# Which operand is held in the array: the product of w_out and phi in an attention, MoE and soft-MoE kernel

## The chip, the cores and the metric

The kernel runs on one core of a Trainium2 chip. The metric is the device time of one execution in microseconds (us); the time before is the median of 3 runs.

## The reference

Three blocks stand one behind the other. The first is causal attention over 4 batches, 12 heads, 448 tokens and a head size of 64. Its result, laid out as x with 1792 rows and 768 columns, goes through a feed-forward block without gates, and its output through a soft mixture of 8 experts with 4 slots each:

```python
h = x @ w_in                      # 768 -> 2048
x = np.maximum(0.01 * h, h) @ w_out   # 2048 -> 768
logits = x @ phi                  # 768 -> 32 slots
d = softmax(logits over tokens); c = softmax(logits over slots)
slot_input = d.T @ x
slot_out = per expert: relu(slot_input @ w1) @ w2
out = c @ slot_out
```

The weights w_in and w_out come in 64-bit floating point and are turned into 32-bit numbers on the chip; everything that the change touches is 32-bit.

## The kernel before, in words

The logits need only `g @ (w_out @ phi)`, so the kernel forms the product `wprime = w_out @ phi` once, 2048 rows by 32 columns, in 16 units f of 128 rows each. A unit is the work of the generator `prep_out`: it takes the raw rows of w_out, converts them on ScalarE, VectorE and GpSimd, stores the converted rows to HBM for a later stage (`wsc`), and turns them with six transposes on TensorE (`wt_ps`, copied by ScalarE to `wt`: six blocks `wt[:, c]` with the model dimension on the partitions). Then come the steps that the change is about. In the kernel before, `phi_sb[:, c]` (128 rows, 32 columns) is the weight and `wt[:, c]` (128 columns) passes through. The six products go to three groups of 32 output partitions, so that three of them can be in the array side by side, two behind each other in each group. That leaves three partial sums of the turned result in `wp_ps` (96 by 128). ScalarE copies them to `w4`. After a `yield AFTER` a further product with `w4` as the weight and a stack of identity blocks passing through adds the three parts and turns the result back (`wf_ps`, 128 by 32), and ScalarE copies it to `wprime[:, f]`.

The order of the work is written by hand on TensorE: every `mm` and `tr` is tied behind the one before, in the order of the program. ScalarE is tied in the same way from the second stage on. The orders of VectorE and GpSimd are left to a planner that works from estimated times. The program runs in stages of 18 slots (`stage`). In each slot one third of the attention of a head pair is issued, then one step of each running generator of the phase BEFORE, then one column block f of the up-projection `H` (18 products, `up`), then one step of each running generator of the phase AFTER, the oldest first. A `yield AFTER` in `prep_out` therefore puts what follows it into the next slot. Units 0 to 9 of w_out are prepared in the third stage (from about 227 to 321 us), units 10 to 15 in the fourth (343 to 432 us).

The tiles of `ps_tr` share one set of PSUM buffers (tag "tr"), two of them in these stages: `wt_ps` (two tiles for a unit), `wp_ps`, `wf_ps`, the turned maxima of the attention (`mps`), its denominators (`dn`), and the logits (`L`). A product into such a tile waits until the buffer's last reader is done. `logits` reads `wprime` as a weight, from about 368 us on. After the fourth stage come the rest of the up-projection with the combination of the logits, and then the expert block, which reads w1 and w2 from HBM.

Of the kernel before, what the change touches and what calls it, by code (L numbers as in the profile page):

```python
# [10 lines left out]
F32 = mybir.dt.float32  # L11
# [23 lines left out]
def tile_attn_moe_softmoe(ctx: ExitStack, tc: tile.TileContext, q, k, v, w_in, w_out, phi, w1, w2, out, dbg=None):  # L35
# [6 lines left out]
    NS = phi.shape[1]  # L42
# [4 lines left out]
    NP = H // 2  # L47
# [12 lines left out]
    istack = const.tile([128, 128], F32, name="istack")  # L60
# [6 lines left out]
    wprime = const.tile([128, NF, NS], F32, name="wprime")  # L67
    phi_sb = const.tile([128, NP, NS], F32, name="phi_sb")
# [19 lines left out]
    def ps_tr(name, shape=(128, 512)):  # L88
        return psum.tile(list(shape), F32, tag="tr", bufs=TR[0], name=name)
# [27 lines left out]
    scalar = Scalar()  # L117
# [13 lines left out]
    mm = partial(in_order, nc.tensor.matmul)  # L131
# [43 lines left out]
    for x, u in enumerate(units):  # L175
        stage = 0 if x < EARLY[0] else 1 if x < whole else 2
        order += [u + (h, stage) for h in ((0, 1) if stage == 2 else (None,))]
    waiting = list(order)
    pools = [None, None, None]
# [34 lines left out]
    def to_f32(u, absmax=None):  # L214

        raw = raws.pop(u)
        kind, f, h, stage = u
        nm = f"{kind}{f}_{h}"
        w = DM if h is None else DH
        hw, lw = raw[..., 1], raw[..., 0]  # L220
        _, nt, ns = BUFS[stage]
        t = pools[stage].tile([128, w], F32, tag="cv_t", bufs=nt, name="cv_" + nm)
        sg = pools[stage].tile([128, w], BF16, tag="cv_s", bufs=ns, name="cs_" + nm)
        ti = t.bitcast(I32)
        scalar.activation(t, hw.bitcast(F32), AF.Abs, scale=2.0**-112)
        scalar.activation(sg, hw.bitcast(F32), AF.Sign)
        if absmax is not None:
            nc.vector.tensor_reduce(absmax, t, AX.X, ALU.max)
        nc.vector.tensor_scalar(ti, ti, 3, None, ALU.logical_shift_left)
        nc.vector.scalar_tensor_tensor(ti, lw, 29, ti, ALU.logical_shift_right, ALU.bitwise_or)  # L230
        load_raw()
        return t, sg
# [28 lines left out]
    def prep_out(us):  # L261

        f, stage = us[0][1], us[0][3]
        wos = []
        for u in us:
            wo, sg = to_f32(u)
            nc.gpsimd.tensor_tensor(wo, wo, sg, ALU.mult)  # L267
            c0 = DH * (u[2] or 0)
            nc.sync.dma_start(
                wsc.rearrange("(k g a p) n -> k a g p n", k=4, g=4, a=4)[f // 4, f % 4][:, :, c0 : c0 + wo.shape[1]], wo  # L270
            )
            wos.append((wo, c0))
            if u is not us[-1]:
                yield BEFORE
        if len(us) == 1:
            yield AFTER
        yield AFTER
        wt = pools[stage].tile([128, NP, 128], F32, tag="wt", bufs=1, name=f"wt{f}")
        for h in (0, 1):
            wo, c0 = wos[h % len(wos)]  # L280
            ps = ps_tr(f"wt_ps{f}_{h}", (128, 3, 128))
            for j in range(3):
                c = 128 * (3 * h + j) - c0
                tr(ps[:, j], wo[:, c : c + 128], ident)
            scalar.copy(wt[:, 3 * h : 3 * h + 3], ps)
            if h == 0 and len(us) > 1:
                yield AFTER
        yield AFTER
        psw = ps_tr(f"wp_ps{f}", (96, 128))
        for c in range(NP):  # L290
            j = c % 3
            mm(
                psw[32 * j : 32 * j + 32], phi_sb[:, c], wt[:, c], start=c < 3, stop=c >= 3, skip_group_check=True
            )
        w4 = pools[stage].tile([96, 128], F32, tag="w4", bufs=1, name=f"w4_{f}")
        scalar.copy(w4, psw)
        yield AFTER
        psf = ps_tr(f"wf_ps{f}", (128, NS))
        mm(psf, w4, istack[:96, :NS], start=True, stop=True)
        scalar.copy(wprime[:, f], psf)  # L300
        ready.add(us[0][:2])

    ready = set()
    BEFORE, AFTER = "before", "after"
# [12 lines left out]
    def prep_start():  # L317
        u = units[started[0]]
        started[0] += 1
        us = [x for x in order if x[:2] == u]  # L320
        g = prep_in(us[0]) if u[0] == "i" else prep_out(us)
        running.append([g, next(g)])
# [557 lines left out]
    if True:  # L880
# [123 lines left out]
        for c in range(4):  # L1004
            wo = loaded.pop(("wo", c))
            for h in range(2):
                for t in range(4):
                    nc.tensor.matmul(
                        psi[h][32 * t : 32 * t + 32], gdt[:, c, t], wo[:, t, 384 * h : 384 * (h + 1)],
                        start=c == 0, stop=c == 3, skip_group_check=True,  # L1010
# [18 lines left out]
        for e in range(E):  # L1029
            ph = ps2(f"ph{e}", (128, 256), tag="h", bufs=4)  # L1030
            for hf in range(2):
                wt = loaded.pop(("w1", (e, hf)))
                for t in range(3):
                    rows = wt[:, t].rearrange("k (p t) -> k p t", t=8)
                    for g in range(4):
# [3 lines left out]
                            start=hf == 0 and t == 0, stop=hf == 1 and t == 2, skip_group_check=True,  # L1039
# [87 lines left out]
        for x, (t0, nt, c0, cols) in enumerate(pieces):  # L1127
            if x:
                load_next(1)
            wt = loaded.pop(("w2", x))  # L1130
# [8 lines left out]
            for h in heads:  # L1139
                for t in range(nt):  # L1140
# [3 lines left out]
                        start=t0 + t < 4, stop=t0 + t >= 8 * E - 4, skip_group_check=True,  # L1144
# [65 lines left out]
```

## Time and profile before

| | |
|---|---|
| median of 3 runs | 646.38 us (645.07 to 647.01) |
| the profiled execution | 642.54 us |
| its span, first to last instruction | 640.8 us |
| mean granted TensorE clock | 0.985 of full speed |
| TensorE products busy (PE) | 573.1 us, 89% |
| weight loads busy (PEld) | 326.0 us, 51% |
| VectorE (DVE) | 382.7 us, 60% |
| ScalarE (ACT) | 289.5 us, 45% |
| GpSimd (POOL) | 238.1 us, 37% |

The profile tells for one execution what each engine did and when. PE is a product's passage, PEld the load of its weight, which can lie beside the product before it. A product of 32-bit numbers appears as two loads and two passages. The duration of a passage contains the way through the array; how closely passages follow each other is read from their starts. A share of busy time is a mean over stages with different limits.

### The profile page before, as it was taken

Reading aid. Unit: us, or ns where it says so; the run is one execution under the profiler, and the core shown is the slowest. Engines: PE = TensorE matmul, PEld = TensorE weight load, DVE = VectorE, ACT = ScalarE, POOL = GpSimd, SP = SyncE. Lnnn points to the kernel's source line nnn. Section 1 sums busy time; section 2 is a strip of 40 time slices with the busy share of each in tenths; the row PEclk is TensorE's granted clock in tenths of the full one; section 3 lists DMA queues with packets and bytes.
Section 4 is the critical chain, followed back from the end, with each engine's and each line's share of the span. In section 5 each row is a group of like instructions: output and inputs, shape, how many; then the busy total and the mean of one; then the engine's idle time right before and its main releaser. Section 6 shows DMA issues by size and latency. Waiting matters only on the chain.

```text
span 640.8 us, 12316 instructions
## 1 busy us (share of the span) xinstructions
PE 573.1 (89%) x4810; PEld 326.0 (51%) x4810; DVE 382.7 (60%) x900; ACT 289.5 (45%) x570; POOL 238.1 (37%) x247
## 2 busy tenths in 40 slices
PE   3688888997899999999999989999999998998564
PEld 2455555654555566555555555554344445554233
DVE  5868757998984666787578778424657423001013
ACT  2566755678665566657445654432022112011012
POOL 5186883388586373444435434430000000000000
PEclk9989989999999999999999999999999998999998
DMA  9942227755662467764343322208969539999999
GB/s 180 288 121 59 60 65 199 216 154 124 163 183 73 86 199 201 202 174 108 98 118 97 111 68 72 61 13 278 358 230 420 202 132 418 410 419 425 408 325 326
DMA packets 123698, 125.68 MB, mean 196 GB/s; under 512 B 84216, under 2 KB 113912, under 8 KB 120056
## 3 DMA queue, kind: packets, MB, share of 16 engines
q1 hardware_dynamic: 123640, 124.90, 61.3%
q8 instruction: 38, 0.62, 0.4%
q14 instruction: 20, 0.16, 0.1%
HBM read 105.74 MB, written 19.14 MB: 195 GB/s over the span
## 4 chain that ended last, share of the span: by engine, by line
PE 61%; DMA 12%; DVE 9%; POOL 9%; ACT 4%; issue 3%; SPq 1%; POOLq 0%; ACTq 0%; DVEq 0%
PE H L102 29%; DMA w<-in_moe_w_dram 8%; PE O L102 5%; PE T L102 4%; PE g_acc L102 3%; PE L L102 2%; PE dn L102 2%; PE S L102 2%; DMA raw_i_None<-in_moe_w_in_dram 2%; DVE cv_i_None L230 2%; PE ph L1036 2%; PE wt_ps L102 2%; POOL tsum L484 2%; ACT P L113 2%; POOL w L258 2%
## 5 line engine op out<-in xcount | busy, mean ns | idle before, releaser
L102 PE MATMUL H<-x,w 128*128 128x448 f16 x1152 | 229.1, 353 | 0.7 <-ACT g L113 0.7
L102 PEld LDWEIGHTS <-w 128*128 128x128 f16 x1152 | 110.1, 99 | 111.7 <-issue 18.2
L435 DVE CUSTOM_DVE_ANT_0 junk<-S,mask 112x224 bf16<-112x224 f32 (+3 forms) x192 | 84.9, 442 | 53.7 <-PE S L102 50.7
L513 DVE RECIPROCAL rs<-rs 128x224 f32<-128x224 f32 x36 | 53.3, 1523 | 25.9 <-ACT rs L113 25.9
L475 POOL TENSOR_SCALAR_AFFINE_SELECT P<-P 112x448 f32<-112x448 f32 x48 | 34.7, 724 | 88.6 <-ACT P L113 52.9
L113 ACT ACTIVATE P<-T 112x672 f32<-112x672 f32 (+1 forms) x72 | 56.9, 792 | 21.2 <-PE T L102 20.2
L102 PE MATMUL T<-qkt 64*112 64x336 f32 (+3 forms) x576 | 59.4, 318 | 4.1 <-ACT P L113 3.3
L113 ACT ACTIVATE g<-H,iv 128x448 f32<-128x448 f32 x48 | 30.4, 634 | 64.2 <-PE H L102 45.8
L102 PE MATMUL O<-P,v 112*64 112x448 f32 (+3 forms) x384 | 54.4, 426 | 3.9 <-POOL P L475 3.9
L102 PEld LDWEIGHTS T<-qkt 64*112 64x112 f32 x576 | 42.2, 178 | 14.2 <-issue 5.7
L484 POOL TENSOR_TENSOR tsum<-tsum,P 112x448 f32<-112x448 f32 (+1 forms) x48 | 47.3, 986 | 1.8
L102 PEld LDWEIGHTS O<-P,v 112*64 112x64 f32 x384 | 26.2, 142 | 29.9 <-issue 13.0
L480 POOL TENSOR_TENSOR tsum<-P 112x672 f32<-112x672 f32 x24 | 39.1, 1630 | 1.8
L102 PE MATMUL S<-qkt 64*112 64x224 f32 (+3 forms) x192 | 31.3, 365 | 8.4 <-DVE mxe L435 3.7
L1028 POOL MEMSET hz<- 128x256 f32 x2 | 0.6, 311 | 97.7 <-PE g_acc L102 97.7
L113 ACT ACTIVATE g_spare<-H,iv 128x448 f32<-128x448 f32 x16 | 10.1, 634 | 56.8 <-PE H L102 56.8
L113 ACT ACTIVATE mr<-mps,own 128x112 fp32r<-128x112 f32 x96 | 26.2, 361 | 16.7 <-PE mps L102 16.7
L113 ACT COPY rs<-dn 128x448 f32<-128x448 f32 x18 | 9.6, 532 | 51.9 <-PE dn L102 51.9
L102 PE MATMUL T<-mr,onesr 64*112 64x448 f32 (+1 forms) x192 | 30.7, 316 | 2.5 <-ACT mr L113 2.5
L249 POOL TENSOR_TENSOR cv_i_None<-cv_i_None,cs_i_None 128x768 f32<-128x768 f32 x16 | 28.5, 1784 | 11.6 <-ACT cs_i_None L113 11.6
L267 POOL TENSOR_TENSOR cv_o_None<-cv_o_None,cs_o_None 128x768 f32<-128x768 f32 x10 | 16.5, 1646 | 40.7 <-DVE cv_o_None L230 21.5
L258 POOL TENSOR_TENSOR w<-cv_i_None,w 128x768 f16<-128x768 f32 x16 | 26.8, 1674 | 10.4 <-ACT w L113 10.4
(179 smaller groups left out, 907.6 us busy)
## 6 DMA issues: line engine op xcount, KB each, us to landing
w<-in_moe_w_dram SPq DMA_DIRECT2D x31, 1536.0 KB, 14.9
raw_i_None<-in_moe_w_in_dram SPq DMA_DIRECT2D x16, 768.0 KB, 4.8
raw_o_None<-in_moe_w_out_dram SPq DMA_DIRECT2D x10, 768.0 KB, 5.7
g_far<-g SPq DMA_DIRECT2D x32, 224.0 KB, 4.3
gb<-g_far SPq DMA_DIRECT2D x8, 896.0 KB, 6.9
wo<-wsc SPq DMA_DIRECT2D x4, 1536.0 KB, 7.7
v<-in_v_dram SPq DMA_DIRECT2D x24, 224.0 KB, 3.5
out_dram<-ob SPq DMA_DIRECT2D x14, 384.0 KB, 3.7
```

The source lines that it names most:

```text
L102: op(*args, **kwargs)
L113: op(*args, **kwargs)
L230: nc.vector.scalar_tensor_tensor(ti, lw, 29, ti, ALU.logical_shift_right, ALU.bitwise_or)
L249: nc.gpsimd.tensor_tensor(t, t, sg, ALU.mult)
L258: nc.gpsimd.tensor_tensor(lo, w, hi, ALU.subtract)
L267: nc.gpsimd.tensor_tensor(wo, wo, sg, ALU.mult)
L435: nc.vector.tensor_tensor_reduce(out=junk[:, :w], in0=ps[:, a, at : at + w], in1=mask[:, S - w :], scale=-1.0, scalar=3e38, op0=ALU.add, o ...
L475: nc.gpsimd.affine_select(out=d, in_=d, compare_op=ALU.is_ge, fill=0.0, base=0, pattern=[[0, 4], [1, CP]], channel_multiplier=-1,)
L480: nc.gpsimd.tensor_tensor(tsum[:CP], p[0][:CP, :, 0, CP:], p[0][:CP, :, 1, : S - CP], ALU.add)
L484: nc.gpsimd.tensor_tensor(y, y, p[1][:CP, :, j, : S - CP * (j + 2)], ALU.add)
L513: nc.vector.reciprocal(rs[:, c : c + S // 2], rs[:, c : c + S // 2])
L1036: nc.tensor.matmul(ph[32 * g : 32 * g + 32].rearrange("s (p u) -> s p u", u=2), sit[:, 3 * hf + t], rows[:, :, 2 * g : 2 * g + 2], start=h ...
```

## The change

The turned block of w_out becomes the weight (128 columns, 32-bit) and `phi_sb[:, c]` (32 columns) passes through. All six products add up in one PSUM tile of 128 by 32, which already has the orientation of `wprime[:, f]`; ScalarE copies it there. The tile `w4`, its copy, the product with the identity stack, the tile `wf_ps` and one `yield AFTER` go.

```diff
         yield AFTER
-        psw = ps_tr(f"wp_ps{f}", (96, 128))
+        psw = ps_tr(f"wp_ps{f}", (128, NS))
         for c in range(NP):
-            j = c % 3
-            mm(
-                psw[32 * j : 32 * j + 32], phi_sb[:, c], wt[:, c], start=c < 3, stop=c >= 3, skip_group_check=True
-            )
-        w4 = pools[stage].tile([96, 128], F32, tag="w4", bufs=1, name=f"w4_{f}")
-        scalar.copy(w4, psw)
-        yield AFTER
-        psf = ps_tr(f"wf_ps{f}", (128, NS))
-        mm(psf, w4, istack[:96, :NS], start=True, stop=True)
-        scalar.copy(wprime[:, f], psf)
+            mm(psw, wt[:, c], phi_sb[:, c], start=c == 0, stop=c == NP - 1)
+        scalar.copy(wprime[:, f], psw)
         ready.add(us[0][:2])
```

## Rows read from the trace of the kernel before

**Rows 1.** Windows: engines' busy us in a stretch (instructions), clock, DMA.

```profile
230.00:290.00 60.00, 57.99 (x463) 34.85 (x463) 42.60 (x82) 37.31 (x78) 28.90 (x24) 1.00 0.65 190
290.00:325.00 35.00, 34.14 (x273) 20.33 (x273) 25.00 (x50) 19.80 (x43) 15.82 (x14) 1.00 0.43 102
...
345.00:385.00 40.00, 38.18 (x305) 22.00 (x304) 30.48 (x69) 23.55 (x52) 18.92 (x19) 1.00 0.28 81
385.00:435.00 50.00, 48.01 (x362) 26.89 (x360) 26.77 (x47) 21.62 (x50) 20.35 (x22) 1.00 0.20 57
```

**Rows 2.** The chain that ended last, in order of time: start, us, what.

```profile
309.73 0.97 PE wt_ps L102 x6
...
565.20 49.82 DMA w<-in_moe_w_dram x2
```

**Rows 3.** Timeline of PE, 231 to 236 us: start, us, instructions merged.

```profile
231.30 3.57 PE L102 MATMUL H<-x,w 128*128 128x448 f16 x18
234.80 0.64 PE L102 MATMUL wp_ps<-wt,phi_sb 128*32 128x128 f32 x12
235.36 0.99 PE L102 MATMUL wt_ps<-ident,cv_o_None 128*128 128x128 f32 x6
236.28 0.36 PE L102 MATMUL S<-qkt 64*112 64x224 f32 x2
```

**Rows 4.** Timeline of PE, 239 to 244 us; in brackets a wait and its releaser.

```profile
239.52 3.57 PE L102 MATMUL H<-x,w 128*128 128x448 f16 x18
242.93 0.31 PE L102 MATMUL wf_ps<-istack,w 96*128 96x32 f32 x2
243.16 0.64 PE L102 MATMUL wp_ps<-wt,phi_sb 128*32 128x128 f32 x12
243.98 0.85 PE L102 MATMUL wt_ps<-ident,cv_o_None 128*128 128x128 f32 x6 [0.18 <-ACT wprime L113]
```

**Rows 5.** Timeline of PE: products of one weight form, two overlapping stretches near 537 us.

```profile
536.15 1.73 PE L102 MATMUL pgt<-istack,ge 128*128 128x32 f32 x14
...
536.82 1.06 PE L102 MATMUL pgt<-istack,ge 128*128 128x32 f32 x8
```

**Rows 6.** Windows: busy PE, PEld, DVE, ACT, POOL of a stretch near 550 us.

```profile
549.00:551.50 2.50, 2.28 (x12) 2.17 (x12) 0.12 (x2) 0.48 (x1) 0.00 (x0) 1.00 0.97 413
```

**Rows 7.** Timeline of PE, 227 to 229 us and 255 to 258 us.

```profile
227.60 0.82 PE L102 MATMUL wt_ps<-ident,cv_o_None 128*128 128x128 f32 x6
228.35 0.71 PE L102 MATMUL T<-qkt 64*112 64x336 f32 x6
...
255.73 0.31 PE L102 MATMUL wf_ps<-istack,w 96*128 96x32 f32 x2
255.87 0.53 PE L102 MATMUL wt_ps<-ident,cv_o_None 128*128 128x128 f32 x3
256.70 0.55 PE L102 MATMUL wt_ps<-ident,cv_o_None 128*128 128x128 f32 x3 [0.30 <-ACT wprime L113]
257.17 0.36 PE L102 MATMUL S<-qkt 64*112 64x224 f32 x2
```

**Rows 8.** Timeline of PE: further turns and products that waited.

```profile
262.09 0.85 PE L102 MATMUL wt_ps<-ident,cv_o_None 128*128 128x128 f32 x6 [0.44 <-ACT w L113]
...
374.60 0.41 PE L102 MATMUL wf_ps<-istack,w 96*128 96x32 f32 x2 [0.44 <-ACT rs L113]
375.68 0.52 PE L102 MATMUL wt_ps<-ident,cv_o 128*128 128x128 f32 x3 [0.67 <-ACT wprime L113]
...
402.66 0.52 PE L102 MATMUL wt_ps<-ident,cv_o 128*128 128x128 f32 x3 [0.43 <-DVE l L126]
```

**Rows 9.** Groups of instructions of ACT: count, busy us, mean ns, idle before.

```profile
L113 ACT COPY w<-wp_ps 96x128 f32<-96x128 f32 x16 | 4.2, 260 | 0.5
...
L113 ACT COPY wprime<-wf_ps 128x32 f32<-128x32 f32 x16 | 2.9, 182 | 0.0
```

**Rows 10.** Groups of PE, 227 to 435 us: the products that waited for POOL.

```profile
L102 PE MATMUL dn<-tsum,onesr 128*64 128x336 f32 x44 | 8.2, 452 | 1.5 <-POOL tsum L484 1.5
```

## The prediction

> **What bounds the kernel now.** I read the busy times by stretch first, since a mean over the whole span hides the stages. In the two stages in which w_out is prepared, TensorE's products are busy for 57.99 of 60, 34.14 of 35, 38.18 of 40 and 48.01 of 50 us, and no other engine passes 77% of its stretch [rows 1]. The reader is to see that all four stretches leave TensorE only 6.7 us without work, at a granted clock of 1.00 (the upper level, 2.4 GHz). Second, the chain of work that ended last: in these stages it runs mostly through TensorE, and a unit's turn is itself a piece of it [rows 2]. Behind them, from 565 us, the chain is the transfer of expert weights, which starts when the up-projection has given its buffers free; so what TensorE loses before 435 us moves the end by as much, unless a wait takes it up. Third, TensorE's timeline around the changed steps, to see how closely their starts follow each other and what they wait for [rows 3, 4, 7, 8].
>
> So the question is TensorE's time for one unit, times 16, and which waits behind these steps go or come.
>
> **What goes.** The old product of a unit takes 12 passages, three side by side. From its first start to the next tile's start are 235.36 - 234.80 = 0.56 us [rows 3]; with ends rounded to 0.01 it may be 0.57, which I take. 16 x 0.57 = 9.1 us. The product with the identity stack: 0.24 us where another old product follows (243.16 - 242.93) [rows 4], 0.14 where a turn follows (255.87 - 255.73) [rows 7]. The trace has six of the first kind, seven of the second, and three that stand apart, which I set at 0.3 each: 6 x 0.24 + 7 x 0.14 + 0.9 = 3.3 us. And a small item: the old product starts 0.07 us before the modelled end of the H products ahead of it (231.30 + 3.57 - 234.80) [rows 3], the full-width identity product 0.16 before (239.52 + 3.57 - 242.93) [rows 4]. A change of the array's division costs 0.09 us; six old products stand directly behind H: 0.5 us. Removed: 9.1 + 3.3 + 0.5 = 12.9 us.
>
> ScalarE's copies of 96 by 128, 16 x 0.26 = 4.2 us, go as well; the copy to wprime, 0.18 us each, stays [rows 9]. ScalarE is busy for 37.31 of 60 us [rows 1], so the copies' own time I cost at nothing; what counts is who waits for them, below. No DMA is issued by the removed step or moved, and the queues of SP and POOL carry on in the same program order.
>
> **What comes.** The new product has 12 passages again, but each with a weight of 128 columns and only 32 columns passing. The trace has this form: the product of `ge` with the identity stack. Two stretches that end together hold 14 and 8 such passages, in 1.73 and 1.06 us, so one costs 0.67 / 6 = 0.112 us [rows 5]. The load sets this, since 32 columns passing cannot cover it. When the first load lies beside the H product ahead, two passages and the step to a turn take 0.14 us [rows 7]; the other ten cost 0.112 each: 0.14 + 1.12 = 1.26 us for a unit, 20.2 us for 16. Six are followed by products on a part of the array (0.09 each, 0.5 us); three stand behind logits, which use column groups (0.09 each), and in about four the first load can't be ahead (0.08 each): 0.6 us. Added: 21.3 us.
>
> The lower bound for a passage is 0.03 us, what the step of 0.14 us for two passages leaves beside one of 0.11 [rows 5, 7]; the upper is 2.28 / 12 = 0.19 us, measured where the weight is read with a step of three elements [rows 6]. The blocks of `wt` are contiguous like those of `ge`, so I take 0.112. The Trainium skill ("TensorE: Matmul & The Clock Gate", section on LDWEIGHTS) prices a load by its columns, columns / 1.2 ns, which makes 107 ns for 128 of them; an estimate by it is 0.8 us less over 160 passages. The trace's 112 ns is what I use.
>
> TensorE's bill before waits: 21.3 - 12.9 = +8.4 us.
>
> **Waits that go.** A buffer of the "tr" set is needed again at once by the next unit's turn. Where the identity product stands directly ahead of a turn, the turn's second half waits until ScalarE, busy with g, has copied wprime: that turn takes 257.17 - 255.87 = 1.30 us, a free one 228.35 - 227.60 = 0.75 [rows 7]. The slot now has no product of this unit, so 0.55 us go, three times: 1.65. Where both products and a turn stand together, the turn waits 0.18 us for the wprime copy [rows 4], twice: 0.36. The three waits of 0.44, 0.67 and 0.43 us behind the maxima and the logits [rows 8] are covered by the longer product or lose their cause: 1.54. Together 3.6 us.
>
> **Waits that come or stay.** A turn behind a product waits for that product's copy with its second half, 0.92 us instead of 0.75 (236.28 - 235.36) [rows 3]; the three pairs freed above now have this: +0.5 us. One of the three identity products that stand apart lies beside the maxima's own copies on ScalarE, which the next product with them needs anyway: +0.3 not gained. Behind the logits it depends on which buffer the turn gets; if it is the product's, its 0.43 us come back. What queues behind such a wait is all of TensorE, whose order is fixed, and then ScalarE's exponentials. Small remainders of 0.03 to 0.07 us at eight turns go the other way, about -0.3.
>
> The sum: 8.4 - 3.6 + 0.8 - 0.3 = +5.3 us. TensorE also waits 1.5 us for GpSimd's sums [rows 10]; a product ahead of these can hide some 0.3 there. I forecast **+5.0 us**: the profiled execution goes from 642.5 to 647.5, and the median, which was 3.8 us above it, from 646.4 to 651.4 us. A measurement of this kernel can tell about 0.3% (1.9 us) from no change.
>
> **The rivals.**
>
> 1. The waits don't go. Sixteen tiles fewer pass through two buffers, so each later tile can meet another holder, a long copy of denominators (0.44 us in [rows 8]) in place of a short one. Then +8.4 + 0.8 = +9.2 us, 655.6 us. For it: the waits of rows 8 name three different holders. Against: the three slots without a product have nothing left to wait for.
>
> 2. The waits take it up. TensorE is without work for 6.7 us of these stretches [rows 1]; less the 3.6 us already counted, 3.1 are left, 1.5 of them for GpSimd [rows 10]. If the later start of TensorE hides all of them, +5.0 - 3.1 = +1.9 us, 648.3, and with a few tenths of luck in the planner's orders no difference. Against: most of them stand ahead of the added work in their slot, or are for ScalarE copies that move with TensorE.
>
> 3. The other side: the loads lie side by side with the passages more than I think. Each passage under 0.112 us saves 160 times the difference; the break-even is 0.112 - 5.0 / 160 = 0.081 us. At 0.03 us, as two starts with loads ahead show, it is 160 x 0.08 = 12.8 us less: -7.8, 638.6 us. Against it stand the 14 passages of the same form, at the full clock [rows 5].
>
> 4. The packing is worth more than I count. The old product has three passages side by side; if the new one costs three times the old, 1.71 us, then 16 x (1.71 - 1.26) = 7.2 us more: +12.2, 658.6 us. With the 0.19 us of rows 6 a passage it would be 16 x 10 x 0.08 = 12.8 us more: +17.8, 664.2. Against both: rows 5. Beside this rival stands a rule of the Trainium skill ("TensorEngine Tiling (Array Packing)", section "When to Use Tiling") that speaks against this change: with 32 columns on the passing side it advises the swap that makes them the weight, with column groups, for up to 4 times the speed. The trace so far shows 0.57 against 1.26 us, 2.2 times.
>
> **How the numbers follow.** My forecast, from +2 to +7: 0.56. Rival 1: 0.14. Rival 2: 0.18, of which 0.13 lies within 0.3% and 0.05 beyond it on the fast side, as the planner's orders of VectorE and GpSimd may shift by a microsecond or two. Rival 3: 0.06. Rival 4: 0.06. Faster by over 0.3%: 0.05 + 0.06 = 0.11. Within: 0.13 and 0.03 from the forecast's lower edge, 0.16. Slower: 0.73. The range leaves out rival 3, the fast end of rival 2 and rival 4, some 0.17: 646.5 to 656.5 us. The sign is fairly sure, so the forecast's own range, 648.5 to 653.5, is the better guide to its size.
>
> **What would show it.** In the profile after: 192 passages into `wp_ps` of 32 columns with 128-column loads, starts some 0.11 us apart, 1.26 us to a following turn; no `wf_ps`, 16 ScalarE copies fewer; turns of 0.75 us in slots without a product; TensorE without work for less of 225 to 440 us than before; the fourth stage's last H some 5 us later, and everything behind it later by the same. Wrong would be: starts under 0.08 us apart, turns that still wait 0.5 us, or a transfer tail that ends at the old time though TensorE is later.

## The result, and the profile after

| | before | after |
|---|---|---|
| median of 12 runs each, taken side by side | 646.24 us | 652.85 us |
| ratio, 95% interval | | 1.0096 (1.0069 to 1.0122) |
| profiled execution's span | 640.8 us | 649.7 us |

Slower by some 6.2 us (4.5 to 7.9), and clear of 0.3%. The ratio is that of the means, 646.75 and 652.95 us; the medians differ by 6.6. The forecast was +5.0 us, 651.4.

Where the time is lost is read by stages. The first two fences are the windows of the third and fourth stage, each from its first H product to that of the stage behind, before and after (columns as in [rows 1]: the stretch, its length, busy PE, PEld, DVE, ACT and POOL, the granted clock, DMA).

```profile
219.18:334.97 115.79, 112.84 (x890) 67.35 (x890) 83.21 (x167) 69.79 (x143) 54.28 (x46) 1.00 0.57 153
334.97:441.05 106.08, 101.55 (x758) 56.86 (x757) 67.24 (x136) 53.50 (x119) 42.13 (x43) 1.00 0.30 81
```

```profile
218.53:337.59 119.06, 117.38 (x870) 74.93 (x869) 82.83 (x167) 68.35 (x133) 54.25 (x46) 1.00 0.55 149
337.59:447.18 109.59, 105.00 (x745) 61.46 (x744) 67.11 (x136) 52.93 (x113) 42.14 (x43) 1.00 0.28 78
```

+3.27 and +3.51 us, 6.78 together, and TensorE's busy time grows by 7.99. The granted clock is 1.00 in both stages of both kernels, so it has no part in this. From the first H behind them (441.05 and 447.18 us) to the first `pgt` (536.02 and 542.14 us) both take 95.0 us, so the delay is carried through whole. The third stage began 0.65 us earlier than before. The spans differ by more, 8.9 us, since the expert block took 104.8 us there in one profiled execution and 107.6 in the other. That difference is not the change's: the experiments below took 104.8 to 107.7 in this block, among them two kernels with the changed product, 104.8 and 107.7. Behind [rows 2] the chain still ends through the expert weights, 7.6 us later, 6.1 of it from the stages:

```profile
572.83 49.69 DMA w<-in_moe_w_dram x2
```

The timeline of TensorE after, for the unit of [rows 3]:

```profile
230.65 3.57 PE L102 MATMUL H<-x,w 128*128 128x448 f16 x18
234.06 1.42 PE L102 MATMUL wp_ps<-phi_sb,wt 128*128 128x32 f32 x12
235.31 0.99 PE L102 MATMUL wt_ps<-ident,cv_o_None 128*128 128x128 f32 x6
236.23 0.36 PE L102 MATMUL S<-qkt 64*112 64x224 f32 x2
```

From the product's first start to the turn's are 1.25 us, where 0.56 were; the product now starts 0.16 us before the modelled end of H, not 0.07. The turn itself still takes 0.92, since its second half waits for the copy, as before. The tile's own row gives the load's and the copy's durations (min, median, max in ns):

```profile
L102 PEld LDWEIGHTS wp_ps<-phi_sb,wt x192: 186/192/192, 233.9 to 434.7; 128*128 128x128 f32 x192
...
L113 ACT COPY wprime<-wp_ps x16: 186/186/188, 235.5 to 435.0; 128x32 f32<-128x32 f32 x16
```

Charging each TensorE instruction of the two stages from its start to the next one's, less waits over 0.07 us, gives the bill:

| us on TensorE, third and fourth stage | before | after | difference |
|---|---|---|---|
| product `wp_ps` | 9.36 | 21.42 | +12.06 |
| identity product `wf_ps` | 3.40 | 0 | -3.40 |
| H, L (change of the array's division) | 114.64 | 114.43 | -0.21 |
| turn `wt_ps`, its short stalls included | 14.27 | 13.60 | -0.67 |
| T | 28.58 | 28.81 | +0.23 |
| waits over 0.07 us | 6.86 | 5.64 | -1.22 |
| sum | | | +6.79 |

The waits went only in part. Where a turn stood behind an identity product [rows 7], it is free, 0.75 us:

```profile
256.56 0.82 PE L102 MATMUL wt_ps<-ident,cv_o_None 128*128 128x128 f32 x6
257.31 0.36 PE L102 MATMUL S<-qkt 64*112 64x224 f32 x2
```

Where the identity product had stood behind the turned maxima, nothing was gained. The next product that needs them now waits 0.64 us for ScalarE, in place of the identity product and its own wait of 0.44; from the maxima to the next S product it is 2.05 us before (first fence) and 2.04 after:

```profile
320.07 0.32 PE L102 MATMUL mps<-ident,mxe 112*128 112x112 f32 x1
320.83 0.41 PE L102 MATMUL wf_ps<-istack,w 96*128 96x32 f32 x2 [0.44 <-ACT rs L113]
...
322.12 0.36 PE L102 MATMUL S<-qkt 64*112 64x448 f32 x2
```

```profile
322.66 0.31 PE L102 MATMUL mps<-ident,mxe 112*128 112x112 f32 x1
322.90 0.86 PE L102 MATMUL T<-qkt 64*112 64x448 f32 x6
324.40 0.46 PE L102 MATMUL T<-mr,onesr 64*112 64x448 f32 x2 [0.64 <-ACT mr L113]
324.70 0.37 PE L102 MATMUL S<-qkt 64*112 64x448 f32 x2
```

Behind the first logits the turn waited 0.52 us before (timeline of all engines):

```profile
369.18 0.61 PE L102 MATMUL wp_ps<-wt,phi_sb 128*32 128x128 f32 x12
...
369.91 0.25 ACT L113 COPY w<-wp_ps 96x128 f32<-96x128 f32 x1
...
370.31 0.52 PE L102 MATMUL wt_ps<-ident,cv_o 128*128 128x128 f32 x3 [0.52 <-POOL tsum L484]
...
371.31 0.61 DVE L126 COPY l<-L 128x448 f32<-128x448 f32 x1
```

The profile names GpSimd's sums as what ended this wait. But of the set's two buffers the logits still held one, since their copy starts only at 371.31 us, so the turn had the buffer of `wp_ps`, which ScalarE's copy freed at 370.16. After the change the turn got the logits' buffer, which VectorE empties late, after its transposes and conversions:

```profile
371.44 0.96 PE L102 MATMUL L<-g,wprime 128*32 128x448 f32 x8
...
372.32 1.52 PE L102 MATMUL wp_ps<-phi_sb,wt 128*128 128x32 f32 x12
...
374.34 0.61 DVE L126 COPY l<-L 128x448 f32<-128x448 f32 x1
...
375.09 0.52 PE L102 MATMUL wt_ps<-ident,cv_o 128*128 128x128 f32 x3 [1.24 <-DVE l L126]
```

Two of the waits in [rows 8] grew shorter but did not go, those of 262.09 and 375.68 us, and have another releaser now:

```profile
262.89 0.88 PE L102 MATMUL wt_ps<-ident,cv_o_None 128*128 128x128 f32 x6 [0.21 <-POOL cv_o_None L267]
...
379.48 0.52 PE L102 MATMUL wt_ps<-ident,cv_o 128*128 128x128 f32 x3 [0.53 <-ACT rs L113]
```

The wait for GpSimd's sums [rows 10] grew, where a part of it should have been hidden:

```profile
L102 PE MATMUL dn<-tsum,onesr 128*64 128x336 f32 x44 | 8.2, 452 | 1.8 <-POOL tsum L476 1.8
```

### The profile page after: what moved, and what is told of

Read it like the earlier page. It is cut to its first block, busy times and chain, and to the rows that moved or that the text cites. A ratio compares the mean times of both kernels' runs of the same rounds, so it can differ in the third digit from the quotient of the medians.

```text
span 649.7 us, 12230 instructions
## 1 busy us (share of the span) xinstructions
PE 583.2 (90%) x4778; PEld 340.9 (52%) x4778; DVE 382.3 (59%) x900; ACT 287.7 (44%) x554; POOL 237.5 (37%) x247
## 4 chain that ended last, share of the span: by engine, by line
PE 64%; DMA 9%; DVE 8%; POOL 8%; ACT 4%; issue 3%; SPq 1%; ACTq 0%; DVEq 0%; POOLq 0%
PE H L102 29%; DMA w<-in_moe_w_dram 8%; PE O L102 5%; PE T L102 5%; PE wp_ps L102 3%; PE g_acc L102 3%; PE dn L102 3%; PE S L102 3%; PE L L102 2%; PE ph L1028 2%; DVE cv_i_None L230 2%; PE wt_ps L102 2%; POOL w L258 2%; ACT P L113 2%; POOL tsum L476 1%
## 5 line engine op out<-in xcount | busy, mean ns | idle before, releaser
L102 PE MATMUL O<-P,v 112*64 112x448 f32 (+3 forms) x384 | 52.4, 413 | 4.4 <-POOL P L467 4.4
L102 PEld LDWEIGHTS O<-P,v 112*64 112x64 f32 x384 | 25.3, 138 | 29.3 <-issue 12.2
```

Of the source, the lines that this page charges most:

```text
L102: op(*args, **kwargs)
```

## The experiments

All are set against the kernel before. The stages are taken as above, from each profile. "The same bill" is the one above, made for another kernel. The two theories: the loads (a passage of the new product costs the load of its 128 columns, and TensorE sets the end), and the waits (the buffers of the turn decide).

| kernel | ratio to before (95%) | third stage | fourth | both, against before |
|---|---|---|---|---|
| before | | 115.79 | 106.08 | |
| changed | 1.0096 (1.0069 to 1.0122) | 119.06 | 109.59 | +6.78 |
| 128 columns pass | 1.0123 (1.0076 to 1.0171) | 119.62 | 109.88 | +7.63 |
| half the product | 0.9984 (0.9955 to 1.0013) | 113.04 | 108.10 | -0.73 |
| product twice | 1.0473 (1.0392 to 1.0554) | 135.02 | 120.69 | +33.84 |
| old, identity product ahead of H | 1.0008 (0.9982 to 1.0033) | 116.39 | 106.22 | +0.74 |
| four column groups | 0.9980 (0.9951 to 1.0008) | 112.77 | 107.94 | -1.16 |
| groups, logits copied by ScalarE | 0.9942 (0.9909 to 0.9975) | 114.30 | 104.34 | -3.23 |
| changed, logits copied by ScalarE | 1.0079 (1.0049 to 1.0109) | 120.53 | 108.15 | +6.81 |
| before, logits copied by ScalarE | 0.9984 (0.9960 to 1.0007) | 115.79 | 105.89 | -0.19 |

**128 columns pass through each weight.**

```diff
-    phi_sb = const.tile([128, NP, NS], F32, name="phi_sb")
+    phi_w = const.tile([128, NP + 3, NS], F32, name="phi_w")
+    nc.gpsimd.memset(phi_w[:, NP:], 0.0)
+    phi_sb = phi_w[:, :NP]
...
-        psw = ps_tr(f"wp_ps{f}", (128, NS))
+        psw = ps_tr(f"wp_ps{f}", (128, 4 * NS))
         for c in range(NP):
-            mm(psw, wt[:, c], phi_sb[:, c], start=c == 0, stop=c == NP - 1)
+            mm(psw, wt[:, c], phi_w[:, c : c + 4].rearrange("p c s -> p (c s)"), start=c == 0, stop=c == NP - 1)
-        scalar.copy(wprime[:, f], psw)
+        scalar.copy(wprime[:, f], psw[:, :NS])
```

> The new product as it is, but 128 columns pass through each weight in place of 32 (three further blocks beside the wanted one, their results unused). If the load of 128 columns sets the pace of a passage (0.112 us), a passage of 128 columns, which the old product shows at about 0.11 us for a round, is covered by it: time as the changed kernel, about +6 us on the kernel before, starts still 0.11 us apart. If the passing columns add to the load, 96 more columns cost about 0.08 us each time: 16 x 12 x 0.08 = 15 us more, about +21 us.

```profile
234.90 1.50 PE L104 MATMUL wp_ps<-phi_w,wt 128*128 128x128 f32 x12
236.24 0.99 PE L104 MATMUL wt_ps<-ident,cv_o_None 128*128 128x128 f32 x6
```

1.34 us to the turn in place of 1.25: four times the columns cost 0.09 us for a unit, about what the first two passages had saved with loads that were ahead. The stages take 0.85 us more than those of the changed kernel. The load sets the pace; 96 further columns pass under it for nearly nothing.

**Half the product.**

```diff
-        for c in range(NP):
-            mm(psw, wt[:, c], phi_sb[:, c], start=c == 0, stop=c == NP - 1)
+        for c in range(NP // 2):
+            mm(psw, wt[:, c], phi_sb[:, c], start=c == 0, stop=c == NP // 2 - 1)
```

> The new product with three of its six blocks left out (half of the sum over the model dimension is missing). If the passages are the price and TensorE sets the end, 16 x 6 x 0.112 = 10.7 us go: about -4.5 us against the kernel before, although the step and the buffers are those of the changed kernel. If the price lies in the new waits behind the product or in the step that went, the time stays near that of the changed kernel, +4 to +6 us.

In the two stages 7.5 us went, not 10.7, and the ratio lies between the two expectations. By the same bill the product costs 10.56 us less than in the changed kernel, but the waits grow by 1.41, and O and S products of the attention, unchanged in number, take 1.63 us more, all of it where the clock has fallen. The third stage gave 6.02 of the 6.7 that are ten units' share; a turn there waits 0.9 us for its converted rows, 0.2 in the changed kernel. The fourth gave 1.5 of 4.0: the turn waits 0.67 us longer for the same late copy, and then the clock falls. The timeline of TensorE, and the window behind it with the granted clock in the third column from the end:

```profile
369.58 0.86 PE L102 MATMUL wp_ps<-phi_sb,wt 128*128 128x32 f32 x6
372.35 0.52 PE L102 MATMUL wt_ps<-ident,cv_o 128*128 128x128 f32 x3 [1.91 <-DVE l L126]
```

```profile
372.80:376.30 3.50, 3.50 (x15) 1.51 (x16) 0.80 (x4) 0.48 (x1) 0.01 (x1) 0.51 0.51 144
```

So the loads theory holds where TensorE sets the pace, and the waits theory at these two turns; the fall of the clock was in neither.

**The product twice.**

```diff
-        for c in range(NP):
+        for c in (*range(NP), *range(NP)):
```

> The new product made twice in a row in each unit (the second time over the first, result the same): 12 passages more, 16 x 12 x 0.112 = 21.5 us of TensorE. If TensorE sets the end in both stages, +19 to +21.5 us from the first turn to the last H products against the changed kernel (up to 2.5 us of waits can be covered). If other engines pace the fourth stage, only the third stage's 13.4 us and a part of the 8.0 show: +15 to +18.

In the stages +27.1 us against the changed kernel, above the 21.5 of either reading (the kernel ran twice only). By the same bill the product itself costs 21.2 us more, as expected, and 2.7 us of waits are covered. The other 8.5 us are O, T, S and dn products of the attention and H products that run longer at unchanged counts. Set against the changed kernel product by product, all of it falls into six stretches in which the granted clock is down to 0.50, and none outside (8.7 and -0.1 us). Windows of the two stages, and of two of those stretches with some time at 1.00 around them:

```profile
219.67:354.69 135.02, 133.62 (x990) 89.95 (x990) 81.46 (x167) 68.32 (x133) 54.59 (x46) 0.97 0.48 131
354.69:475.38 120.69, 118.68 (x817) 73.14 (x816) 66.86 (x136) 52.94 (x113) 42.26 (x43) 0.94 0.26 71
...
277.00:281.50 4.50, 4.50 (x36) 3.39 (x36) 0.94 (x3) 2.79 (x6) 2.38 (x3) 0.62 0.55 206
...
407.50:411.50 4.00, 4.00 (x33) 3.12 (x32) 0.92 (x5) 2.36 (x5) 2.06 (x2) 0.57 0.18 49
```

The clock stood at 1.00 in both stages of the changed kernel.

**The identity product ahead of H**, in the kernel before:

```diff
         scalar.copy(w4, psw)
-        yield AFTER
+        yield BEFORE
```

> The kernel before, with one word changed: the identity product is issued in the phase BEFORE of the next slot, ahead of the H products, in place of AFTER. If the waits that the prediction counted are those of the turn behind it, the three turns of 1.30 us and the two waits of 0.18 us go and one of 0.67: -2 to -2.7 us against the kernel before. If they only move to the next holder of the two buffers, no difference (within 1 us).

No gain: +0.74 us in the stages, the ratio holds 1. The three turns of 1.30 us are gone from the timeline, as are the two waits of 0.18, but the product now meets the denominators' buffer three times in the third stage, where it had once before, each like this:

```profile
240.25 0.32 PE L102 MATMUL mps<-ident,mxe 112*128 112x112 f32 x1
241.00 0.41 PE L102 MATMUL wf_ps<-istack,w 96*128 96x32 f32 x2 [0.44 <-ACT rs L113]
241.25 3.57 PE L102 MATMUL H<-x,w 128*128 128x448 f16 x18
```

What goes at the turns comes back for the most part at the next holder, and the wait of 0.67 us stays: the waits over 0.07 us are only 0.25 us less in all (6.86 and 6.61). The turns' short stalls give another 0.47, but the identity product itself (+0.77), the maxima (+0.34) and H (+0.46) cost more in the new order. So the waits move, the rival's reading, for this move.

**Four column groups.**

```diff
         for c in range(NP):
-            mm(psw, wt[:, c], phi_sb[:, c], start=c == 0, stop=c == NP - 1)
+            for j in range(4):
+                r = slice(32 * j, 32 * j + 32)
+                mm(psw[r], wt[:, c, r], phi_sb[:, c], start=c == 0, stop=c == NP - 1, skip_group_check=True)
```

> The new product, each block cut into four weights of 32 columns in four column groups (48 passages for a unit in place of 12, result the same). If the loads of different column groups lie side by side, as the starts of the old product 0.007 us apart suggest, a round of four costs 0.04 to 0.06 us and a unit 0.5 to 0.7: 9 to 12 us less than the changed kernel, -3 to -6 us against the kernel before. If loads are served one behind the other by their columns, 12 rounds cost at least what 12 loads of 128 cost: +6 to +9 us.

```profile
234.31 0.63 PE L102 MATMUL wp_ps<-phi_sb,wt 128*32 128x32 f32 x48
234.87 0.89 PE L102 MATMUL wt_ps<-ident,cv_o_None 128*128 128x128 f32 x6
...
367.63 0.60 DVE L126 COPY l<-L 128x448 f32<-128x448 f32 x1
...
368.38 0.52 PE L102 MATMUL wt_ps<-ident,cv_o 128*128 128x128 f32 x3 [2.21 <-DVE l L126]
```

48 passages take 0.56 us to the turn, as long as the old product, with the result in the new orientation and no second product. By the same bill the product costs 12.2 us less than in the changed kernel, about the upper end of what was expected, but in the two stages only 7.9 us go; the ratio to the kernel before is not clear of 1, since the waits are 2.3 us more, 2.21 us being now spent in the one for the logits' buffer (fence above), and the clock falls behind it (0.98 in the fourth stage), which costs O and dn products 1.6 us.

**The first logits copied by ScalarE**, in three kernels; `tied[0]` is not yet set in the fourth stage, so that only the copy for batch 2 changes its engine:

```diff
-            vector.tensor_copy(l4s[b], ps)
+            (vector.tensor_copy if tied[0] else scalar.copy)(l4s[b], ps)
```

With the groups: 

> The product in four column groups, and the first logits of batch 2 copied out of their buffer by ScalarE in place of VectorE. If the turn's wait of 2.2 us behind the first logits is a wait for VectorE's late copy, it goes: 2 us less than the groups alone from the first turn to the last H, about -3 us against the kernel before. If the turn waits for something else as well (its converted rows), less than 1 us.

```profile
366.45 0.53 ACT L113 COPY l<-L 128x448 f32<-128x448 f32 x1 [1.97 <-PE L L102]
...
367.13 0.52 PE L102 MATMUL wt_ps<-ident,cv_o 128*128 128x128 f32 x3 [0.29 <-ACT l L113]
```

The wait falls from 2.21 to 0.29 us, the fourth stage from 107.94 to 104.34, and the kernel is faster than the one before: 0.9942 (0.9909 to 0.9975), a median of 641.0 us beside 645.4. Of the 3.6 us, 1.9 are the wait, and most of the rest is the fall of the clock (1.6), which did not come behind it this time; one came in the third stage instead (0.99), which is 1.5 us longer than with the groups alone.

With the changed kernel: 

> The changed kernel with the same ScalarE copy of the first logits. If the 1.24 us at that place is a wait for VectorE's copy, about 1.1 us less than the changed kernel in the fourth stage, so that +5 to +5.5 us are left; the passages' own price stays.

The fourth stage lost 1.44 us. The third was 1.47 longer, with the same instructions on TensorE; two windows of it, ahead of and in the slow stretch:

```profile
261.00:264.70 3.70, 3.03 (x29) 2.23 (x26) 3.65 (x8) 1.71 (x6) 1.64 (x1) 1.00 0.72 166
264.70:268.10 3.40, 3.40 (x17) 2.24 (x16) 2.30 (x4) 1.39 (x3) 0.00 (x0) 0.50 0.79 157
```

The ratio, 1.0079, leaves most of the loss in place. With the kernel before: 

> The kernel before with the same ScalarE copy, as a control. Its turn waited there for another buffer's copy (0.52 us), so the logits' copy was not in its way: within 1 us of the kernel before.

 The ratio holds 1, and the stages differ by 0.19 us: the late copy was in the way only of the new arrangements, in which the turn has the logits' buffer. Beside this control the groups with the same copy are ahead by 3.0 us in the stages, but the intervals of the two ratios still overlap a little.

## Why the prediction was right

**The loads.** The step that carried the sign, a passage priced by `ge`'s product at 0.112 us [rows 5], held: 1.25 us for a unit, forecast 1.26. Passing four times as many columns for 0.09 us shows that it is the load and not the passing; and a fixed price for each change of weight, whatever its width, is not it either, since each of the four column groups takes twelve weights of 32 columns in 0.56 us. The bill before waits was forecast at +8.4 us; the rows of `wp_ps`, `wf_ps`, H and L give 12.06 - 3.40 - 0.21 = +8.45. In the 128-column form the starts are (1.50 - 0.28) / 11 = 0.111 us apart, where 0.28 is the last passage's own duration. The rule of the Trainium skill ("TensorE: Matmul & The Clock Gate", LDWEIGHTS) puts a load of 128 columns at 107 ns, some 4 ns below that; the measured spacing decides.

**TensorE sets the end.** Right: the 6.78 us of the stages reach the expert block undiminished, and twelve more passages cost their full 21.2 us. Rival 2, that waits take it up, fails in the changed kernel; in half the product, with less to do, waits do take up 1.4 of the 10.6 us.

**The waits**, a net -3.4 us with the share hidden behind GpSimd, is the term that was mis-sized: the turns, T and waits together gave 0.67 - 0.23 + 1.22 = 1.66 us. Three parts of it went astray. Of the turns behind logits the prediction had weighed only one, its 0.43 us gone or back; that one went. Another, behind the first logits, had waited 0.52 us before and now waits 1.24, as the logits' own buffer fell to it: 0.7 us that no term held. GpSimd's sums were waited for 0.35 us longer, not 0.3 less. And of the 1.54 us counted for the waits of [rows 8], 1.25 went: the turn of 262.09 us still waits 0.21 of its 0.44, and the one of 375.68 us waits 0.53, where it and the identity product ahead of it had waited 0.67 and 0.44. The term of the maxima came true: 0.3 us were not gained there. So did what was counted as gone for certain, the three long turns and the two waits of 0.18. Two turns that wait over 0.5 us are one of the signs that the prediction named for being wrong, and they mark this term. Rival 1 named the mechanism; it came true by half.

**Rivals 3 and 4.** A passage of the 128-column weight does not go under 0.11 us. The 0.19 us that rival 4 took from [rows 6] contains the last passage's own duration; six starts there, from 549.06 to 550.13 us, are 0.178 apart, so its second price was set too high. But the reasoning of rival 3, loads side by side, is true of column groups, and there the loss is gone: four groups make the swapped product as cheap as the old one. Beside it stands the rule of the Trainium skill ("TensorEngine Tiling (Array Packing)", "When to Use Tiling"), which advises the swap with column groups for a passing side of 32: the old form had 0.56 us, and so has the form with the weight cut into four, so the trace agrees on the groups, and shows that the swap is not needed for them.

**What stays open.** Why the buffer that falls to the turn changed when one tile in six went: the order of release is the planner's, and only its outcome was seen. Why GpSimd's sums were waited for longer was not tested. Whether falls of the clock in the third stage come more often with the new product: of seven profiles without the identity product three have one or two (between 260 and 268 us with the ScalarE copies, near 278 and 295 us with the product twice), of three with it none, too few to tell.

## What to carry to other kernels

In a stretch that TensorE fills, count passages by what sets their pace: a full-width 32-bit weight with few columns passing costs its load, so making the larger operand the weight can double a product's price although one product fewer is made. If the orientation is wanted, cut the weight into column groups, so that loads lie side by side. And before counting a wait as gone, look for the next holder of the same buffer.

## What was not expected of the hardware

Four loads of 32 columns in different column groups with their passages take far less than one load of 128 columns: 48 of them with their passages 0.56 us, 12 full loads 1.25.

TensorE's granted clock fell to half, its 1.2 GHz level, inside stretches without long idle time. Half the product shows 0.51 from 372.8 to 376.3 us, behind six narrow passages and a wait of 1.91 us; the changed kernel with ScalarE's copy 0.50 from 264.7 to 268.1 us, behind a wait, twelve narrow passages and another wait, where the same instructions on TensorE in the changed kernel kept 1.00; the doubled product fell six times. One such fall made the stage some 1.5 us longer, a quarter of the whole effect under study. Read the clock before comparing two profiles' stages.
